# QKV stage of a fused block kernel: Y rows saved one at a time, x statistics one pass later, first z block's casts later, two tiles interleaved at the start

## The chip, the cores and the metric

One core of a Trainium2 chip runs the whole kernel. The metric is the device time of one execution in microseconds (us), lower is better. Engines are named as in the profile: PE is TensorE (matmuls and transposes), DVE is VectorE, ACT is ScalarE, POOL is GpSimd, and SP is SyncE, whose queue issues nearly all DMA transfers of this stage. Each engine works through its own instructions in program order.

## The reference, cut to what matters

```python
x = A_x                                    # 2048 tokens x 576
xn = _layernorm(x)
qkv = xn @ wqkv                            # 576 x 1728: the QKV stage
A = local_dilated_attention(qkv) @ wo      # 32 heads, window 8, dilation 2
h  = _gelu(_layernorm(xn) @ w1)            # the mixing stage's first matmul
x1 = xn + shift_mix(h) @ w2
B  = x1 + _gelu(_layernorm(x1) @ w3) @ w4  # 576 -> 4608 -> 576
return x + A + B
```

The change touches only the normalisation of x, the product with wqkv, and the preparation of z, the second normalisation of x, for the w1 product that follows.

## The kernel before, in words

Every float32 product is made from rounded parts: an operand is cast to a high part ("hi", by ACT), the rest is found by subtraction ("lo", by DVE), and hi·hi, hi·lo and lo·hi are summed in PSUM. The instruction order of each engine is the order of the Python statements; there is no scheduler. Tokens come in 16 tiles of 128. `Y[:, t, :]` holds tile t of x, and its normalised form overwrites it.

**Start.** `load_x(t)` and `load_cg(cg, ...)` put x tiles and column groups of wqkv (288 columns each) on SP's queue. For each tile `stats_x(t)` (DVE L110 to L112, then a power on POOL, L113), `norm_x(t)` (DVE L120) and `tails(t)` (POOL L292: a copy of the last columns) give the normalised tile; `turn_x(t)` and `turn_tail(t)` (PE L300, L304) transpose it, `cast_x` makes hi (ACT L311) and lo (DVE L312). The weight group is split by `hi_main` (ACT L251), `lo_main` (DVE L254) and `split_tail` (ACT L259, lo at L260). `q_head(t)` is the first 12 of a tile's 14 matmuls (PE L393), `q_tail(t)` the last two and the copy out by ACT (`q_leave`, L398). Within the 14, the first six need hi of x and of the weights and the first half of the weights' lo, numbers 6 and 7 the second half of that lo, 8 to 11 the lo of x, and the last two the tails of both.

**Units.** Then 36 units of 14 matmuls run, each a tile times a column group (`q_plain`), numbered as in `units`; the table `plan` attaches preparation work to unit numbers. Each unit's result takes one of two PSUM banks until ACT has copied it out.

**Passes.** Tiles 6 to 15 are done in five passes p = 3 to 7 of two tiles each, with a seven-product scheme: per pass three column groups of seven steps, so 21 steps, numbered 0 to 20 (the last pass has 23), each of seven matmuls (`seven`, L596). `plan[k]` holds what is issued after step k. Results leave through `leave`: ACT copies them (L605) into one of five `stg` buffers, or DVE adds them (L607) to one of five `keep` buffers (which ACT filled before, L623 and L629), and SP sends each buffer to `qkvd` (L381). While pass p computes, pass n = p + 1 is prepared: `low2` after step 3 and `up2` after step 7 transpose the two next tiles on PE (L300, L304) and form their sums, on ACT (L354) and DVE (L356, L361 to L363). The scratch space of those sums is three rows of Y, given by `raw_s`:

```python
t = {3: 13, 4: 13, 5: 0, 6: 5, 7: 5}[p]
return (Y[:, t:t + 3, :].rearrange("p a c -> p (a c)")[:, :1536]
```

So the sums of pass 5 overwrite rows 0 to 2 of Y, and those of passes 6 and 7 rows 5 to 7. These rows hold normalised x that is needed later; `away(k0, k1)` sends them to DRAM (`ysp`, L562) before, and after the pass 7 sums `back` reads them again. The same table also places `z_turn(t)` (ACT L557 scales the tile into z, DVE L129 and L130 transpose it into the one tile `ST`) and, after four of them, `put(("z", b))`: four DMAs of ST to DRAM (L137). In pass 7 `get(("z", 0))` reads the first z block (L142), `split_x` casts it (ACT L149, L150, L155) and finds its lo (DVE L151, L156), and `split_w1` splits a slice of w1 (L168, L169). The mixing stage's matmuls (L734) begin right after pass 7.

Of the kernel before, what the change touches and what calls it, by code (L numbers as in the profile page):

```python
# [8 lines left out]
F32 = mybir.dt.float32  # L9
# [48 lines left out]
def fused_block(ctx, tc, x, wqkv, wo, w1, w2, w3, w4, out):  # L58
# [188 lines left out]
    def flat(v):  # L247
        return v.rearrange("p o s c -> p o (s c)")
# [4 lines left out]
    def lo_main(raw, b, o, k):  # L253
        dve.tensor_tensor(WB[b][:, o + k, 1:3, :], raw[:, k, 1:3, :],  # L254
                          WB[b][:, o + k, 3:5, :].bitcast(F32), op=ALU.subtract)
# [46 lines left out]
    def turn_tail(t, ps):  # L302
        for k in range(2):
            pe.transpose(ps[:, k, 0:128], tl[t][:, 128 * k:128 * (k + 1)], ident)  # L304
# [23 lines left out]
    def plain_x(t):  # L328
        return x_ops(("q", t // 4)), 2 * (t % 4)
# [102 lines left out]
    for i in range(24):  # L432
# [8 lines left out]
    x0 = plain_x(0)[0]  # L441
# [63 lines left out]
    def upper(p):  # L505
# [149 lines left out]
    for p in range(3, 8):  # L655
        n = p + 1
        if n < 8:
            q4 = 4 * (p - 3)
            zs = (q4 + 1, q4 + 2, q4 + 3, q4) if p == 4 else range(q4, q4 + 4)
            plan = {k: ((z_turn, t),) for k, t in zip((9, 10, 16, 17), zs)}  # L660
            plan.update({0: ((norm_x, 2 * n),), 2: (), 3: ((low2, n),), 4: ((tails, 2 * n),),
                         7: ((up2, n),), 8: ((lambda n=n: cast_upper(n, two[n]),),),
                         14: ((cast_s, n, 0),), 15: ((cast_s, n, 1), (cast_s, n, 2))})
            plan[17] += ((put, ("z", p - 3)),)
            if n < 7:
                plan[2] = ((stats_x, 2 * n + 3),)
                plan[4] += ((stats_x, 2 * n + 2),)
                plan[17] += ((norm_x, 2 * n + 3), (tails, 2 * n + 3))
            plan[11] = {3: ((scales, 4, 6),), 4: ((away, 5, 8), (scales, 8, 10)),
                        5: ((load_w1,), (scales, 12, 14)), 6: ()}[p]  # L670
            plan[18] = {3: ((load_x, 13), (load_x, 12), (away, 0, 3)),
                        4: ((load_x, 15), (load_x, 14), (away, 3, 5))}.get(p, ())
        else:
            zx = xring
            plan = {3: ((lambda: get(("z", 0), ring_block(("z", 0))),),),
                    12: ((lambda: split_x(zx["z", 0], 2),),),
                    14: ((open_w1,), (split_w1, 0)),
                    15: ((lambda: split_x(zx["z", 0], 3),),),
                    18: ((lambda: split_x(zx["z", 0], 1),),)}
# [1061 lines left out]
```

## Time and profile before

| | |
|---|---|
| three runs | 1305.28, 1302.47, 1303.38 us; median 1303.38 us |
| profiled execution | 1301.31 us, span 1299.5 us |
| mean granted TensorE clock | 0.988 |
| PE busy | 1265.0 us, 97% of the span |
| DVE, ACT, POOL busy | 72%, 59%, 20% of the span |
| QKV stage | from the start to 214.39 us, where the mixing stage's first matmul starts |

The profile's second part cuts the span into 40 slices of about 32 us and gives each engine's busy share in tenths. PE has its only clear dips in the first slice and in the slices from 97 to 162 us, all in the QKV stage. The view of waits sums up, for each engine, what released it after idle time; the timeline gives single instructions with their start, duration and the idle time before them; the view of windows gives busy times, granted clock and DMA traffic in a stretch. In a row such as `[7.54 <-DVE Y L356]` the engine had stood idle for 7.54 us until line 356 on DVE had finished. For SP the second column is the time from the first issue to the end of the last.

### The profile page before, as it was taken

The page shows a single profiled execution, that of the slowest core. Times are in us where ns is not written, and L with a number is a line of the kernel's source. Part 1 is how long each engine was busy: PE and PEld are TensorE (multiplying, and loading weights), DVE is VectorE, ACT ScalarE, POOL GpSimd, SP SyncE. Part 2 cuts the span into 40 slices and gives each one's busy share as a digit, 9 for nine tenths or more (in the row PEclk, how much of TensorE's full clock was granted, in tenths as well). Part 3 has the DMA queues.
Part 4 walks back from the last instruction along what each step waited for, and adds up shares of the span by engine and source line. Part 5 has one row for each costly group of instructions (what it writes and reads, how often), then busy time and mean ns, then how long its engine had stood idle before and what let it go on. Part 6 is the DMA issues. An engine that isn't in the chain of part 4 may idle for free.

```text
span 1299.5 us, 21014 instructions
## 1 busy us (share of the span) xinstructions
PE 1265.0 (97%) x7819; PEld 1166.5 (90%) x7819; DVE 932.0 (72%) x1205; ACT 765.2 (59%) x1276; POOL 264.5 (20%) x408
## 2 busy tenths in 40 slices
PE   7997899999999999999999999999999999999999
PEld 7997898899889899999889999999989999999898
DVE  5875554677738798999557998998998884455341
ACT  3554455634644554554767777777757777677730
POOL 2212100011132121112113322222123223222100
PEclk9998899999999999999999999999999999999999
DMA  6736687536788879668849889878957868899982
GB/s 183 180 84 145 170 189 182 162 100 175 193 215 190 204 152 214 123 150 202 195 84 219 181 182 225 179 153 200 282 99 164 168 125 166 187 220 214 255 254 82
DMA packets 208654, 228.92 MB, mean 176 GB/s; under 512 B 80920, under 2 KB 142328, under 8 KB 208424
## 3 DMA queue, kind: packets, MB, share of 16 engines
q1 hardware_dynamic: 175800, 160.79, 43.3%
q0 software_dynamic: 32752, 66.80, 31.9%
q8 instruction: 61, 1.00, 0.3%
q14 instruction: 41, 0.34, 0.1%
HBM read 127.71 MB, written 110.23 MB: 183 GB/s over the span
## 4 chain that ended last, share of the span: by engine, by line
PE 64%; DVE 2%; ACT 2%; DMA 1%; issue 1%; SPq 0%; DVEq 0%; ACTq 0%
PE ps L1139 31%; PE cc L1401 19%; PE p L1103 9%; PE ps L183 4%; DMA td0T<-xn 1%; DVE po L1017 1%; DMA xt<-xn 1%; DVE xt L868 0%; DVE w3st L1236 0%; DVE c L1097 0%; PE p L1708 0%; ACT Y L1144 0%; ACT xt L1198 0%; DVE L L1020 0%; DVE Y L1150 0%
## 5 line engine op out<-in xcount | busy, mean ns | idle before, releaser
L1139 PEld LDWEIGHTS ps<-w,c 128*128 128x128 f32 x3456 | 478.7, 189 | 22.3 <-ACT ev L1144 2.2
L1139 PE MATMUL ps<-w,c 128*128 128x288 f32 x3456 | 489.7, 297 | 6.6 <-ACT ev L1144 2.0
L1145 POOL DMA_DIRECT2D yd<-Y x154 | 138.0, 899 | 395.6 <-ACT Y L1144 327.6
L1097 DVE TENSOR_TENSOR c<-Y,c 128x512 fp32r<-128x512 f32 x144 | 98.8, 687 | 97.2 <-ACT Y L1086 95.8
L1144 ACT COPY Y<-ps 128x576 f32<-128x576 f32 x154 | 97.8, 636 | 76.2 <-PE ps L1139 66.0
L1401 PE MATMUL cc<-xt,w3s 128*128 128x512 f32 (+1 forms) x504 | 127.7, 393 | 1.0 <-DVE Y L1411 1.0
L1401 PEld LDWEIGHTS cc<-xt,w3s 128*128 128x128 f32 (+1 forms) x504 | 92.2, 188 | 19.1 <-DVE Y L1411 1.4
L1147 ACT COPY Y<-ps 128x576 f32<-128x576 f32 x92 | 58.9, 640 | 66.3 <-PE ps L1139 64.8
L1401 PE MATMUL cc<-x1n,w3a 128*128 128x512 f32 (+1 forms) x336 | 86.7, 397 | 0.5 <-ACT cc L1604 0.5
L1017 DVE TENSOR_TENSOR po<-q,k 128x1152 f32<-128x1152 f32 (+1 forms) x48 | 84.2, 1755 | 1.0
L1020 DVE TENSOR_REDUCE L<-po 128x64 f32<-128x1152 f32 (+1 forms) x48 | 84.0, 1750 | 0.8
L1085 ACT ACTIVATE c<-p 128x512 fp32r<-128x512 f32 x48 | 28.6, 597 | 86.7 <-PE p L1103 86.6
L1411 DVE TENSOR_TENSOR Y<-cc,Y 128x512 f32<-128x512 f32 x49 | 33.7, 687 | 59.2 <-ACT Y L1407 55.1
L993 DVE TENSOR_TENSOR po<-v,L 128x1152 f32<-128x1152 f32 x56 | 75.4, 1353 | 0.9
L393 PE MATMUL p<-wb,xt 128*128 128x288 f32 (+1 forms) x504 | 72.2, 302 | 0.1
L1401 PEld LDWEIGHTS cc<-x1n,w3a 128*128 128x128 f32 (+1 forms) x336 | 61.3, 190 | 12.0 <-ACT cc L1604 0.7
L393 PEld LDWEIGHTS p<-wb,xt 128*128 128x128 f32 (+1 forms) x504 | 69.0, 192 | 1.2 <-DVE xt L449 0.3
L596 PE MATMUL ca<-wb,xt 128*128 128x288 f32 x420 | 64.4, 305 | 3.7 <-DVE keep L607 2.9
L997 DVE TENSOR_TENSOR po<-po 128x1152 f32<-128x1152 f32 x49 | 66.4, 1355 | 0.9
L596 PEld LDWEIGHTS ca<-wb,xt 128*128 128x128 f32 x420 | 60.6, 198 | 4.4 <-DVE keep L607 3.4
L1120 ACT COPY ps<-Y 128x576 f32<-128x576 f32 x92 | 59.4, 646 | 4.4 <-DVE Y L1150 2.3
L113 POOL TENSOR_TENSOR rs<-rs,mhalf 128x1 f32<-128x1 f32 x32 | 18.8, 588 | 200.5 <-DVE mv L116 109.8
(256 smaller groups left out, 2155.8 us busy)
## 6 DMA issues: line engine op xcount, KB each, us to landing
yd<-Y POOLq DMA_DIRECT2D x156, 288.0 KB, 6.1
Y<-in_B_w_dram SPq DMA_DIRECT2D x29, 576.0 KB, 6.0
w3st<-in_B_w_dram SPq DMA_DIRECT2D x56, 256.0 KB, 8.0
qkvd<-stg SPq DMA_DIRECT2D x66, 144.0 KB, 2.9
yd<-ev POOLq DMA_DIRECT2D x26, 288.0 KB, 6.5
w3st<-in_B_w_dram SPq DMA_DIRECT2D x92, 64.0 KB, 7.9
xd<-st SPq DMA_DIRECT2D x16, 320.0 KB, 4.9
xd<-big SPq DMA_DIRECT2D x16, 320.0 KB, 7.3
```

The source lines that it names most:

```text
L393: pe.matmul(ps[:, :QB], xo[:n, o + k, a, :], W[:n, w + k, v, :], start=i == 0, stop=i == len(PLAIN) - 1)
L596: pe.matmul(ps[:, :QB], xo[:n, XO[x], a, :], W[:n, OP[w], v, :], start=start and i == 0, stop=stop and i == len(HALVES) - 1, skip_group_ch ...
L993: dve.tensor_tensor(dst, vv, Lf[:, :, w:w + 1].to_broadcast([128, TPP * GH, HD]), op=ALU.mult)
L997: dve.tensor_tensor(o, o, dst, op=ALU.add)
L1017: dve.tensor_tensor(dst, qf[:, None, :].to_broadcast([128, n, TPP * GC]), win, op=ALU.mult)
L1020: dve.tensor_reduce(Lw[:, w:w + n, :], dst.rearrange("p w (x d) -> p w x d", d=HD), axis=AX.X, op=ALU.add)
L1097: dve.tensor_tensor(h[:, 1, :], g, h[:, 0, :].bitcast(F32), op=ALU.subtract)
L1103: pe.matmul(ps, W3[f][:, w, :], x1n[b][:, a, :], start=n == 0, stop=n == len(PAIRS) - 1)
L1139: pe.matmul(ps[:, k, :HF], h[:, col], w[:, p, k * HF:(k + 1) * HF], start=n == 0 and not seed, stop=n == len(seq) - 1, skip_group_check=True)
L1144: act.copy(e.rearrange("p (h c) -> p h c", h=2), ps[:, :, :HF])
L1145: pool.dma_start(yd[t], e, accum_op=ALU.add)
L1401: pe.matmul(ps, WX[w][:k, v, SLOT[w], :], area[sb][xk][:k, a, :], start=onto is None and i == 0, stop=last and i == len(HALVES) - 1, skip_ ...
```

## The change

1. *Start.* The second half of the first weight group's lo moves from DVE to POOL, `stats_x(2)` moves ahead of tile 1's lo on DVE, and the matmuls of tiles 0 and 1 are interleaved: six and six, the tail transposes, then the rest. `turn_tail(2)` moves behind the matmuls of tile 2.
2. *Units 29 to 34.* The splits of two weight groups that stood behind units 34 and 35 move to 29 and 31, and the casts of pass 3's sums one unit later.
3. *Passes 3 to 6.* Every row of Y gets its own `away`, placed after its `z_turn`, in pass 3 for rows 0 to 2 and in pass 4 for 5 to 7. The statistics of the next x tiles move from steps 2 and 4 to step 11 and to step 2 of the pass that follows, and their normalisation with them. Pass 6 sends its z block after step 14, not 17.
4. *Pass 7.* The casts of the first z block move from steps 12, 15 and 18 to 15, 17 and 20.

```diff
-    act.copy(flat(x0[:, 0:2, 3:5, :]), turns[0][:, :, 128:384])
+    cast_x(0)
     hi_main(r0, 0, 0, 1)
-    lo_main(r0, 0, 0, 1)
-    dve.tensor_tensor(flat(x0[:, 0:2, 1:3, :]), turns[0][:, :, 128:384],
-                      flat(x0[:, 0:2, 3:5, :]).bitcast(F32), op=ALU.subtract)
+    lo_main(r0, 0, 0, 1, pool)
+    stats_x(2)
     cast_x(1)
-    pq = {}
+    split_tail(r0, 0, 0, pool)
+    pq = {t: psa.tile([128, 512], F32, name="p1", tag="a") for t in range(2)}
...
-    q_head(0)
-    turn_tail(0, turns[0])
-    turn_tail(1, turns[1])
-    split_tail(r0, 0, 0, pool)
-    cast_x(0, True)
-    cast_x(1, True)
-    q_head(1)
+    for t in range(2):
+        q_part(pq[t], t, 0, 0, 6)
+    for t in range(2):
+        turn_tail(t, turns[t])
+        cast_x(t, True)
+    q_part(pq[0], 0, 0, 8, 12)
+    q_part(pq[0], 0, 0, 6, 8)
+    q_part(pq[1], 1, 0, 6, 12)
     load_cg(1, raw_rows(10))
-    stats_x(2)
     norm_x(2)
     tails(2)
+    stats_x(3)
     q_tail(0)
     turn_x(2)
-    stats_x(3)
     q_tail(1)
     cast_x(2)
-    turn_tail(2, turns[2])
     norm_x(3)
     tails(3)
     q_head(2)
+    turn_tail(2, turns[2])
...
-            28: ((stats_x, 9),), 29: ((norm_x, 9), (load_x, 10)),
-            30: ((lambda: cast_upper(3, two[3]),),), 31: ((cast_s, 3, 0),),
-            32: ((cast_s, 3, 1),), 33: ((cast_s, 3, 2), (stats_x, 8)),
-            34: ((split_t, 2, False),), 35: ((split_t, 2, True),)}
+            28: ((stats_x, 9),), 29: ((split_t, 2, False), (load_x, 10)),
+            30: ((lambda: cast_upper(3, two[3]),), (norm_x, 9)), 31: ((split_t, 2, True),),
+            32: ((cast_s, 3, 0),), 33: ((cast_s, 3, 1),), 34: ((cast_s, 3, 2), (stats_x, 8))}
...
-            plan = {k: ((z_turn, t),) for k, t in zip((9, 10, 16, 17), zs)}
-            plan.update({0: ((norm_x, 2 * n),), 2: (), 3: ((low2, n),), 4: ((tails, 2 * n),),
...
-            plan[17] += ((put, ("z", p - 3)),)
+            for k, t in zip({3: (9, 10, 14, 17), 6: (9, 10, 11, 14)}.get(p, (9, 14, 16, 17)),
+                            (q4 + 1, q4 + 2, q4 + 3, q4) if p == 4 else range(q4, q4 + 4)):
+                at(k, z_turn, t)
+            at(14 if p == 6 else 17, put, ("z", p - 3))
+            if p > 3:
+                at(0, norm_x, 2 * n + 1)
+                at(0, tails, 2 * n + 1)
+                at(2, stats_x, 2 * n)
+            at(3, low2, n)
+            at(4, norm_x, 2 * n)
+            at(4, tails, 2 * n)
...
             if n < 7:
-                plan[2] = ((stats_x, 2 * n + 3),)
-                plan[4] += ((stats_x, 2 * n + 2),)
-                plan[17] += ((norm_x, 2 * n + 3), (tails, 2 * n + 3))
-            plan[11] = {3: ((scales, 4, 6),), 4: ((away, 5, 8), (scales, 8, 10)),
-                        5: ((load_w1,), (scales, 12, 14)), 6: ()}[p]
-            plan[18] = {3: ((load_x, 13), (load_x, 12), (away, 0, 3)),
-                        4: ((load_x, 15), (load_x, 14), (away, 3, 5))}.get(p, ())
+                at(11, stats_x, 2 * n + 3)
...
+            if p == 3:
+                for t, k in enumerate((9, 10, 14)):
+                    at(k, away, t, t + 1)
+                at(11, scales, 4, 6)
+                at(18, load_x, 13)
+                at(18, load_x, 12)
+            if p == 4:
+                for t, k in ((5, 9), (6, 14), (7, 16)):
+                    at(k, away, t, t + 1)
+                at(17, away, 3, 5)
...
-                    12: ((lambda: split_x(zx["z", 0], 2),),),
-                    14: ((open_w1,), (split_w1, 0)),
-                    15: ((lambda: split_x(zx["z", 0], 3),),),
-                    18: ((lambda: split_x(zx["z", 0], 1),),)}
+            at(14, open_w1)
+            at(14, split_w1, 0)
+            at(15, lambda: split_x(xring["z", 0], 2))
+            at(17, lambda: split_x(xring["z", 0], 3))
+            at(20, lambda: split_x(xring["z", 0], 1))
```

The changed text shifts the lines of the passes: L562 becomes L560, L596 L594 and L607 L605.

SP's queue around the end of pass 3, before (`xd<-st` is the put of a z block, `Y<-in_A_x_dram` the loads of x tiles 13 and 12, `ysp0` to `ysp2` the rows 0 to 2 of Y, `stg` and `keep` results on their way to `qkvd`):

```order
L381 DMA qkvd_85<-stg_1278 128x4x72
L381 DMA qkvd_85<-keep_1199 128x4x72
L381 DMA qkvd_85<-stg_1324 128x4x72
L381 DMA qkvd_85<-keep_1258 128x4x72
L381 DMA qkvd_85<-stg_1369 128x4x72
L137 DMA xd_1389<-st_1148 32x20x128 x4
L381 DMA qkvd_85<-keep_1292 128x4x72
L210 DMA Y_71<-in_A_x_dram 128x576 x2
L562 DMA ysp0_1161<-Y_71 128x576
L562 DMA ysp1_1162<-Y_71 128x576
L562 DMA ysp2_1163<-Y_71 128x576
L381 DMA qkvd_85<-stg_1418 128x4x72
```

and now:

```order
L381 DMA qkvd_85<-stg_1268 128x4x72
L560 DMA ysp0_1161<-Y_71 128x576
L560 DMA ysp1_1162<-Y_71 128x576
L381 DMA qkvd_85<-keep_1193 128x4x72
L381 DMA qkvd_85<-stg_1321 128x4x72
L381 DMA qkvd_85<-keep_1248 128x4x72
L560 DMA ysp2_1163<-Y_71 128x576
L381 DMA qkvd_85<-stg_1371 128x4x72
L137 DMA xd_1387<-st_1148 32x20x128 x4
L381 DMA qkvd_85<-keep_1283 128x4x72
L210 DMA Y_71<-in_A_x_dram 128x576 x2
L381 DMA qkvd_85<-stg_1410 128x4x72
```

The three rows of Y now stand ahead of the four z DMAs instead of behind the x loads; the x loads keep their place.

DVE from the end of pass 3 into pass 4, before (`pp` is the PSUM tile of the next tiles' transposes; the L110 rows are the statistics of x tile 13):

```order
L607 TENSOR_TENSOR keep_1292<-cc0_1159,keep_1292 128x288
L607 TENSOR_TENSOR keep_1349<-ca1_1336,keep_1349 128x288
L120 TENSOR_SCALAR Y_71<-Y_71,mv0_77,rs0_80 128x576
L110 BN_STATS bn_83<-Y_71 128x6 x2
L111 BN_AGGR mv0_77<-bn_83 128x2
L112 TENSOR_SCALAR rs0_80<-mv0_77 128x1
L323 TENSOR_TENSOR xt_1483<-pp_1475,xt_1483 128x256
L325 TENSOR_TENSOR xt_1483<-pp_1475,xt_1483 32x128
L356 TENSOR_TENSOR Y_71<-pp_1475,Y_71 128x384
```

and now (the first L110 rows are those of tile 10, which was loaded long before):

```order
L605 TENSOR_TENSOR keep_1351<-ca1_1333,keep_1351 128x288
L120 TENSOR_SCALAR Y_71<-Y_71,mv0_77,rs0_80 128x576
L110 BN_STATS bn_83<-Y_71 128x6 x2
L111 BN_AGGR mv0_77<-bn_83 128x2
L112 TENSOR_SCALAR rs0_80<-mv0_77 128x1
L323 TENSOR_TENSOR xt_1477<-pp_1469,xt_1477 128x256
L325 TENSOR_TENSOR xt_1477<-pp_1469,xt_1477 32x128
L356 TENSOR_TENSOR Y_71<-pp_1469,Y_71 128x384
L605 TENSOR_TENSOR keep_1381<-cc1_1350,keep_1381 128x288
L120 TENSOR_SCALAR Y_71<-Y_71,mv0_77,rs0_80 128x576
```

The rows read alike, but another tile stands in them: what DVE needs ahead of L323 no longer comes from the x loads that end pass 3, and tile 13's statistics follow after step 11.

PE at the start, before (the banks `p_223` and `p_246` belong to tiles 0 and 1, `p_300` to tile 2; `ps<-ident,stg` are the tail transposes):

```order
L393 MATMUL p_223<-wb_116,xt 128x288 x12
L304 MATMUL ps<-ident,stg 128x128 x4
L393 MATMUL p_246<-wb_116,xt 128x288 x12
L393 MATMUL p_223<-wb_116,xt 128x288 x2
L300 MATMUL ps<-ident,Y 128x128 x4
L393 MATMUL p_246<-wb_116,xt 128x288 x2
L304 MATMUL ps<-ident,stg 128x128 x2
L393 MATMUL p_300<-wb_116,xt 128x288 x12
```

and now (`p_230` and `p_231` are tiles 0 and 1, `p_298` tile 2):

```order
L393 MATMUL p_230<-wb_116,xt 128x288 x6
L393 MATMUL p_231<-wb_116,xt 128x288 x6
L304 MATMUL ps<-ident,stg 128x128 x4
L393 MATMUL p_230<-wb_116,xt 128x288 x6
L393 MATMUL p_231<-wb_116,xt 128x288 x6
L393 MATMUL p_230<-wb_116,xt 128x288 x2
L300 MATMUL ps<-ident,Y 128x128 x4
L393 MATMUL p_231<-wb_116,xt 128x288 x2
L393 MATMUL p_298<-wb_116,xt 128x288 x12
L304 MATMUL ps<-ident,stg 128x128 x2
```

The count of matmuls is the same; the two tiles alternate, and tile 2's tail transposes stand behind its twelve matmuls.

More of the change, by code (lines that the diff above doesn't have):

```diff
@@ L656, in fused_block, with at @@
         n = p + 1
+        plan = {k: () for k in range(23)}
+        def at(k, f, *args):
+            plan[k] += ((f,) + args,)
         if n < 8:
             q4 = 4 * (p - 3)
-            zs = (q4 + 1, q4 + 2, q4 + 3, q4) if p == 4 else range(q4, q4 + 4)
-            plan = {k: ((z_turn, t),) for k, t in zip((9, 10, 16, 17), zs)}
-            plan.update({0: ((norm_x, 2 * n),), 2: (), 3: ((low2, n),), 4: ((tails, 2 * n),),
-                         7: ((up2, n),), 8: ((lambda n=n: cast_upper(n, two[n]),),),
-                         14: ((cast_s, n, 0),), 15: ((cast_s, n, 1), (cast_s, n, 2))})
@@ new lines, in fused_block @@
+            at(14 if p == 6 else 17, put, ("z", p - 3))
[6 more added lines that the diff above has]
+            at(4, tails, 2 * n)
+            at(7, up2, n)
+            at(8, lambda n=n: cast_upper(n, two[n]))
+            if n < 7:
+                at(11, stats_x, 2 * n + 3)
+            at(14, cast_s, n, 0)
+            at(15, cast_s, n, 1)
```

18 lines of the change are left out of this document (13 added, 5 removed).

## The prediction

> **What bounds the kernel now.** First the page's strip of slices, then PE's waits, then windows over the places that the waits name, then the timeline of each engine there. The strip shows PE full except at the start and in the fourth and fifth slices, where the granted clock dips:
>
> ```profile
> PE   7997899999999999999999999999999999999999
> PEclk9998899999999999999999999999999999999999
> ```
>
> PE's waits up to 215 us (total, times, longest):
>
> ```profile
> PE pp L300 <- DVE Y L356: 12.4, 2, 7.5
> PE ps L304 <- DVE xt L312: 3.0, 2, 1.8
> PE ca L596 <- DVE keep L607: 2.9, 2, 2.6
> PE ps L300 <- DVE Y L120: 2.1, 2, 1.7
> PE ca L596 <- ACT cb L617: 0.8, 1, 0.8
> ```
>
> All five lie in the QKV stage, and the change touches each. After it PE hardly waits, so time won here should carry to the end. Windows from `low2` to `low2` (passes 3, 4, 5; columns: length, then busy us and instructions of PE, PEld, DVE, ACT, POOL, then clock, DMA share, GB/s):
>
> ```profile
> 91.64:111.61 19.97, 19.97 (x155) 19.97 (x154) 15.10 (x36) 11.51 (x27) 5.07 (x14) 1.00 0.37 81
> 111.61:142.90 31.29, 23.75 (x161) 23.54 (x160) 15.08 (x35) 11.43 (x27) 5.07 (x14) 0.84 0.69 174
> 142.90:170.94 28.04, 23.18 (x161) 22.97 (x160) 15.00 (x35) 11.60 (x27) 5.08 (x14) 0.88 0.83 203
> ```
>
> The first is undisturbed: 155 PE instructions in 19.97 us, so 161 take 20.74 us. Pass 4 loses 31.29 - 20.74 = 10.55 us, pass 5 7.30 us, the slow clock after each wait included. Who waits, in the timelines of SP, DVE, ACT and PE:
>
> ```profile
> 107.74 4.12 SPq L137 DMA_DIRECT2D xd<-st  x4
> 113.73 2.32 SPq L210 DMA_DIRECT2D Y<-in_A_x_dram  x2
> 116.09 1.43 SPq L562 DMA_DIRECT2D ysp<-Y  x3
> 118.89 1.01 SPq L381 DMA_DIRECT2D qkvd<-keep  x1
> 118.03 0.82 DVE L110 BATCH_NORM_STATS2 bn<-Y 128x6 f32<-128x288 f32 x2 [8.64 <-DMA Y<-in_A_x_dram]
> 121.29 0.48 ACT L354 COPY Y<-pp 128x384 f32<-128x384 f32 x1 [9.09 <-DMA ysp<-Y]
> 123.70 1.09 PE L300 MATMUL pp<-ident,Y 128*128 128x128 f32 x4 [7.54 <-DVE Y L356]
> 149.56 0.82 DVE L110 BATCH_NORM_STATS2 bn<-Y 128x6 f32<-128x288 f32 x2 [8.87 <-DMA Y<-in_A_x_dram]
> ```
>
> The z block's DMAs hold SP; the x loads leave 6 us late, the rows of Y behind them 8 us late. DVE stands at the statistics until 118.03, ACT at L354 until the rows have left at 121.29; L356 needs both, and PE's next transposes need the PSUM tile that L356 reads. Pass 5 repeats it with the x load alone.
>
> **Passes 4 and 5.** Both causes go. The rows leave in steps 9 to 14 of pass 3, ahead of the z DMAs, some 10 us before L354. Tile 13's statistics stand after step 11: `low2` of pass 4 starts at 111.61, step 11 ends 8 steps of 0.93 us (pass 7, below) and two transpose groups later; the undisturbed window has 20 steps and two groups, so a group takes (19.97 - 18.66) / 2 = 0.65 us. That is 120.4, and the load had landed by 118.03. What is late next: spills. Without three rows ahead of it the `keep` of 118.89 leaves at 117.5; it lands 3.3 us later, at 120.8:
>
> ```profile
> qkvd<-keep SPq DMA_DIRECT2D x30, 144.0 KB, 3.3
> xd<-st SPq DMA_DIRECT2D x16, 320.0 KB, 4.9
> ```
>
> ACT wants that buffer again at the end of step 10, 119.4, and PE the bank that it copies from at step 13, at 121.3: with the 0.4 us copy no idle, 0.9 if the landing counts from the row's end. In pass 7 ACT waited 1.55 us for such a buffer with PE going on (row below). I take 0.7 us per pass, nearer the second reading because SP is busy with three kinds of transfer, and as bounds 0 and, for slow landings, 2. Gain: 9.85 + 6.6 = 16.45 us.
>
> **Pass 7.**
>
> ```profile
> 187.17 2.97 PE L596 MATMUL ca<-wb,xt 128*128 128x288 f32 x21
> 189.97 2.03 PE L596 MATMUL cc<-wb,xt 128*128 128x288 f32 x14
> 204.85 2.05 PE L596 MATMUL ca<-wb,xt 128*128 128x288 f32 x7 [2.62 <-DVE keep L607]
> 214.39 0.86 PE L734 MATMUL ps<-xt,W 128*128 128x512 f32 x3
> 197.75 0.40 ACT L623 COPY keep<-cc 128x288 f32<-128x288 f32 x1 [1.55 <-DMA qkvd<-keep]
> 202.97 0.61 ACT L149 CAST xt<-xt 64x512 fp32r<-64x512 f32 x1 [2.16 <-DMA xt<-xd]
> 207.23 1.05 ACT L155 CAST xt<-xt 128x1024 fp32r<-128x1024 f32 x1
> 208.31 1.23 DVE L156 TENSOR_TENSOR xt<-xt 128x1024 fp32r<-128x1024 f32 x1 [2.27 <-ACT xt L155]
> ```
>
> Three steps take 189.97 - 187.17 = 2.80 us. Pass 7 starts one step after 187.17, at 188.10; 23 steps end at 209.55, and the mixing stage starts at 214.39: 4.85 us lost, around a 2.62 us wait for the z block. The casts now stand three steps later (2.8 us), and the put ahead of the read leaves three steps earlier, so the block is there. Next in line is DVE: after step 17 come 0.45 us (ACT's copy), the 1.05 us cast, the 1.23 us subtraction and two adds of 0.45, 3.65 us, and PE wants the second add's bank after three steps, 2.8 us. That leaves 0.9 us (0 to 1.5). Gain 3.95 us. The matmul row after 2.62 us of idle took 2.05 us, not 1.1. [...]
>
> **Start.**
>
> ```profile
> 7.62 0.87 POOL L292 COPY stg<-Y 128x256 f32<-128x256 f32 x1 [0.38 <-DVE Y L120]
> 9.62 1.41 POOL L260 TENSOR_TENSOR wb<-rawa,wb 32x576 fp32r<-32x576 f32 x1 [1.14 <-ACT wb L259]
> 14.73 0.40 POOL L292 COPY stg<-Y 128x256 f32<-128x256 f32 x1 [0.68 <-DVE Y L120]
> 7.76 0.68 ACT L251 CAST wb<-rawa 128x576 fp32r<-128x576 f32 x1
> 9.75 0.68 DVE L312 TENSOR_TENSOR xt<-ps,xt 128x512 fp32r<-128x512 f32 x1
> 12.11 0.82 DVE L110 BATCH_NORM_STATS2 bn<-Y 128x6 f32<-128x288 f32 x2
> 14.72 0.66 PE L300 MATMUL ps<-ident,Y 128*128 128x128 f32 x4 [1.70 <-DVE Y L120]
> 17.75 3.01 PE L393 MATMUL p<-wb,xt 128*128 128x288 f32 x12
> 22.85 1.44 PE L393 MATMUL p<-wb,xt 128*128 128x288 f32 x9
> ```
>
> The moved weight subtraction (128x576) has no row on POOL. Near end 1.41 us, L260's time with as many elements per partition; far end four times that, 5.64, if POOL's time went with partitions. DVE takes 0.75 us for both shapes, so I take 1.41: from 8.5, after the cast and the copy, to 9.9. Statistics of tile 2 on DVE now run from about 8.9 to 10.15, the power (0.55) ends at 10.75, the weights' tail (1.41) at 12.15. Interleaving lets six matmuls of tile 1 fill PE while POOL works; both heads end near 12.2. Then the last two matmuls of tile 0; normalisation of tile 2 (after tile 1's lo and the tails) ends near 12.3, and its transposes start at 12.5, not 14.72. Copies out and the cast follow on ACT to 14.4, so tile 2's twelve start at 14.45, not 17.75. With 3.01 us as before, then transposes, cast and lo of tile 3 (0.6, 0.6, 0.7) and its tails, tile 3's matmuls start at 19.85 instead of 22.85; with a full clock at 18.9. Gain 3.3 us, bounds 4.1 and, at 5.64 us on POOL (weights' tail at 16.4), -1.4.
>
> The copy at 7.62, issued beside a DVE subtraction with both inputs in SBUF, took 0.87 us against 0.40 later. [...]
>
> **Units 29 to 35.**
>
> ```profile
> 81.26 0.41 ACT L398 COPY stg<-p 128x288 f32<-128x288 f32 x1
> 87.13 1.43 DVE L254 TENSOR_TENSOR wb<-rawb,wb 128x576 fp32r<-128x576 f32 x2
> 77.41 10.49 PE L393 MATMUL p<-wb,xt 128*128 128x288 f32 x77
> ```
>
> A split (1.43 + 0.75 us on DVE, 1.9 on ACT) now precedes pass 3's upper sums and another stands ahead of unit 32's copy; the copy of 81.26 (unit 31) becomes about 1 us later, and unit 33 needs its bank: 35 of the 77 matmuls after 77.41, at 82.1. I charge 0.8 us (0 to 1.5), and credit the 0.8 us wait for L617, which stood behind those splits, and charge 0.1 us for tile 8's later normalisation. Net -0.1.
>
> **Sum.** 16.45 + 3.95 + 3.3 - 0.1 = 23.6 us off the profiled 1301.31 gives 1277.7. That execution is 2.1 us below the median of its runs; by the median it is 1279.8. I say 1279.
>
> **Rivals.**
> (A) As summed: 1279, by itself 1275 to 1283.
> (B) DMA becomes the limit of passes 4 and 5. Packet time is 0.83 x 28.04 = 23.3 us in pass 5, to fit into 20.74: 2.6 us too much, which at pass 7's rate (4.85 lost for 2.62 waited) costs 4.8; pass 4 has 0.69 x 31.29 = 21.6 less the three rows moved out, so only the 2 us bound. Loss against A 4.1 + 1.3, so 1284. Against: pass 5's w1 load can lag without harm.
> (C) POOL's subtraction goes with partitions: start -1.4 instead of 3.3, 1284.
> (D) Slower: the z put reads the one tile ST, and `z_turn` at step 9 of the next pass must wait for it, DVE's adds behind it. The put has 13 steps and two transpose groups, 13.4 us; it takes 4.12 + 4.9 = 9 us. Idle begins when denser traffic stretches that 1.5 times; for a loss passes 4 to 6 must each lose 8 us, a put of 21 us, 2.3 times. The packet time above exceeds the pass by 1.13 at most. 1306 there.
> (E) Everything is won, no new waits: 10.55 + 7.30 + 4.85 + 4.1 + 0.8 = 27.6, 1274 to 1275.
>
> **Numbers.** A 0.65, B 0.17, C 0.08, D 0.06, E 0.04. The time is A's. The range runs from E's 1274 to B's and C's upper part, 1288. Differences under 0.2% (2.6 us) can't be told from no change. Faster: all but D and a hundredth between, 0.93; same 0.01; slower 0.06.
>
> **What would show it.** In the profile after: no wait of PE over 2 us for L356 in passes 4 and 5, `low2` to `low2` 20.7 to 22 us at a clock above 0.95; ACT waiting for `qkvd<-keep` in passes 4 and 5; the mixing stage some 23 us earlier, under 1 us of PE idle in pass 7; tile 3's matmuls near 19.5 us; the POOL subtraction near 1.4 us. I am wrong if statistics at step 11 still wait for x loads, if PE idles behind ACT's L605 or L629, or if later stages show new PE waits that eat the gain.

## The result and the profile after

The changed kernel takes 1280.95 us (median of four runs, 1279.85 to 1285.26), the kernel before in the same session 1302.93 us (1301.42 to 1305.28): a ratio of 0.984, 95% interval 0.981 to 0.986. Five more runs in a later session gave a median of 1282.25 us and a ratio of 0.985 (0.982 to 0.987). The forecast was 1279 us, with 1274 to 1288 as its range.

The strip of slices and the longest of PE's waits up to 215 us (one of 1.4 us at the very beginning, in both kernels, left out), in the profile after (span 1278.1 us; lines after the change stand two lower in this stage, so L596 is now L594, L607 is L605, L617 is L615, L623 is L621, L629 is L627, L562 is L560):

```profile
PE   8999899999999999999999999999999999999998
PEclk9999999999999999999999999999999999999999
```

```profile
PE ca L594 <- ACT keep L627: 3.5, 1, 3.5
PE p L393 <- ACT xt L311: 1.0, 1, 1.0
PE ps L304 <- POOL rs L113: 0.8, 1, 0.8
```

The waits for L356 are gone. The largest that is left is one wait of 3.5 us, behind a copy into a `keep` buffer. The windows say in which pass (from `low2` to `low2` of passes 3, 4 and 5, then pass 6 to the first matmul of pass 7, then pass 7 to the mixing stage; same columns as before):

```profile
88.11:108.63 20.52, 20.40 (x155) 19.96 (x154) 14.40 (x34) 11.47 (x27) 5.82 (x14) 1.00 0.47 122
108.63:129.88 21.25, 21.12 (x161) 20.86 (x160) 14.79 (x35) 11.56 (x27) 6.35 (x14) 1.00 0.97 209
129.88:156.47 26.59, 22.89 (x161) 22.44 (x160) 14.86 (x35) 11.36 (x27) 3.51 (x9) 0.94 0.93 217
156.47:174.02 17.55, 17.44 (x133) 17.18 (x132) 11.74 (x25) 10.49 (x24) 2.02 (x6) 1.00 0.82 169
174.02:196.42 22.40, 21.71 (x164) 21.46 (x162) 6.99 (x11) 10.16 (x22) 0.14 (x2) 1.00 0.94 200
```

Pass 4 fell from 31.29 to 21.25 us. Pass 5 hardly moved: 26.59 after 28.04. Of its 5.85 us over the undisturbed 20.74, PE stood idle for 26.59 - 22.89 = 3.70, and most of the rest is the slow clock that followed (0.50 from 143.88 to 147.29; in the repeat below the pass took 156.76 - 129.96 = 26.80 us). Place by place, against the prediction's terms (the start by tile 3's matmuls, the units by the first transposes of `low2`):

| term | forecast gain | measured |
|---|---|---|
| start | 3.3 | 22.85 - 19.54 = 3.31 |
| units 29 to 35 and pass 3 | -0.1 | 3.53 - 3.31 = 0.22 in the units, 19.97 - 20.52 = -0.55 in pass 3 |
| pass 4 | 9.85 | 31.29 - 21.25 = 10.04 |
| pass 5 | 6.6 | 28.04 - 26.59 = 1.45 |
| pass 6 | 0 | 17.16 - 17.55 = -0.39 |
| pass 7 | 3.95 | 26.29 - 22.40 = 3.89 |
| to the mixing stage's start | 23.6 | 214.39 - 196.42 = 17.97 |

The row for the start rests on tile 3's matmuls, in the changed kernel:

```profile
19.54 4.73 PE L393 MATMUL p<-wb,xt 128*128 128x288 f32 x33
```

So the forecast of the time was better than its sum, by luck: the stage gave 5.6 us less than summed. The profiled time fell by 21.5 us, of which 3.4 us came behind the start of the mixing stage (1085.1 us from there to the end, now 1081.7), where nothing was changed. Two questions were left: what holds pass 5, and whose those 3.4 us are. Here is pass 5, from the timelines of SP, ACT and PE of the changed kernel:

```profile
126.61 4.15 SPq L137 DMA_DIRECT2D xd<-st  x4
130.81 3.61 SPq L560 DMA_DIRECT2D ysp<-Y  x2
134.51 0.41 SPq L381 DMA_DIRECT2D qkvd<-keep  x1
134.97 1.34 SPq L210 DMA_DIRECT2D Y<-in_A_x_dram  x2
136.88 0.45 SPq L381 DMA_DIRECT2D qkvd<-keep  x1
137.92 0.40 ACT L621 COPY keep<-cc 128x288 f32<-128x288 f32 x1 [3.02 <-DMA qkvd<-keep]
143.19 0.40 ACT L627 COPY keep<-ca 128x288 f32<-128x288 f32 x1 [3.15 <-DMA qkvd<-keep]
143.65 3.56 PE L594 MATMUL ca<-wb,xt 128*128 128x288 f32 x14 [3.46 <-ACT keep L627]
```

The change puts the last two rows of Y, 3 and 4, directly behind the z block's four DMAs in SP's queue (step 17 of pass 4), where they had stood behind the x loads; the list of changes further up does not name this move. SP is busy with the block and these rows from 126.61 to 134.42, and the transfer of a `keep` buffer to `qkvd` (called a spill below) comes out behind them. ACT, which wants the buffers again, waits twice for 3 us: at 137.92 for the spill of 134.51, and at 143.19 for that of 136.88. Only the second wait holds PE, and its spill is slow as well as late: 6.3 us from its issue to the copy behind it, where the prediction's row had a median of 3.3 us from issue to landing.

### The profile page after: what moved, and what is told of

It reads as the page before. It is cut to its first block, busy times and chain, and to the rows that moved or that the text cites. A ratio compares the mean times of both kernels' runs of the same rounds, so it can differ in the third digit from the quotient of the medians.

```text
span 1278.1 us, 21013 instructions
## 1 busy us (share of the span) xinstructions
PE 1258.9 (99%) x7819; PEld 1159.5 (91%) x7819; DVE 930.2 (73%) x1204; ACT 766.7 (60%) x1276; POOL 268.3 (21%) x409
## 4 chain that ended last, share of the span: by engine, by line
PE 62%; DMA 3%; ACT 3%; DVE 2%; issue 1%; SPq 1%; DVEq 0%; ACTq 0%; POOLq 0%
PE ps L1165 30%; PE cc L1427 19%; PE p L1129 9%; PE ps L183 4%; DMA xt<-td1T 1%; DMA x1n<-xn 1%; DMA td0T<-xn 1%; DVE po L1043 1%; DVE xt L894 0%; DVE w3st L1262 0%; ACT Y L1170 0%; PE p L1734 0%; DVE c L1123 0%; ACT Y L1112 0%; ACT xt L1224 0%
## 5 line engine op out<-in xcount | busy, mean ns | idle before, releaser
L1170 ACT COPY Y<-ps 128x576 f32<-128x576 f32 x154 | 98.0, 637 | 75.0 <-PE ps L1165 65.4
L594 PE MATMUL ca<-wb,xt 128*128 128x288 f32 x420 | 62.9, 301 | 4.2 <-ACT keep L627 3.5
L594 PEld LDWEIGHTS ca<-wb,xt 128*128 128x128 f32 x420 | 58.9, 193 | 4.8 <-ACT keep L627 3.7
```

What stands on the lines that cost most here:

```text
L594: pe.matmul(ps[:, :QB], xo[:n, XO[x], a, :], W[:n, OP[w], v, :], start=start and i == 0, stop=stop and i == len(HALVES) - 1, skip_group_ch ...
L1170: act.copy(e.rearrange("p (h c) -> p h c", h=2), ps[:, :, :HF])
```

## The experiments

Two theories of pass 5: Q, the place of the two rows in SP's queue makes the spills late, and the five `keep` buffers turn that into idle PE; D, the prediction's rival B, the DMA engines are simply full (a share of 0.93 to 0.97 in the windows), wherever a transfer stands. All edits are against the changed kernel unless said.

**Rows 3 and 4 elsewhere.**

```diff
             if p == 4:
-                at(17, away, 3, 5)
...
             if p == 5:
-                at(11, load_w1)
+                at(9, away, 3, 4)
+                at(14, away, 4, 5)
...
             if p == 6:
+                at(9, load_w1)
```

The w1 load moves along, from pass 5 into pass 6; the next experiment leaves it in place.

> Rows 3 and 4 of Y leave in pass 5 (steps 9 and 14) instead of pass 4's step 17, and the w1 load stands in pass 6. Theory Q (the two rows behind the z block in SP's queue make pass 5's spills land late, ACT waits for a keep buffer, PE for ACT): pass 5, 26.59 us in the changed kernel, falls to 21.4 to 22.5; pass 4 stays at 21.25 within 0.3; pass 6 (17.55) stays or grows by at most 0.5; the time is 4 to 5 us under the changed kernel's 1281, so 1276 to 1277. Rival D (the core's DMA engines are simply full in passes 4 to 6, wherever a row stands): the loss moves on, pass 5 shrinks but pass 6 or 7 grows by as much, and the time stays within 1.5 us of 1281.

Its passes 4 and 5 in windows:

```profile
108.55:129.81 21.26, 21.14 (x162) 20.88 (x160) 14.78 (x35) 11.52 (x27) 6.36 (x14) 1.00 0.98 209
129.81:151.92 22.11, 21.39 (x162) 20.94 (x161) 14.85 (x35) 11.43 (x27) 3.50 (x9) 1.00 0.94 194
```

Pass 5 took 22.11 us instead of 26.59, and passes 6 and 7 together 40.18 instead of 39.95: the loss is gone, not moved on. The DMA share of pass 5 is what it was (0.94). The time was 1277.35 us (1276.19 to 1280.62; ratio to the kernel before 0.981, 0.979 to 0.984). Q's numbers, not D's.

**The same bytes in another order.**

```diff
-                at(17, away, 3, 5)
                 at(18, load_x, 15)
                 at(18, load_x, 14)
+                at(19, away, 3, 4)
+                at(20, away, 4, 5)
```

> Rows 3 and 4 leave at steps 19 and 20 of pass 4, behind the two x loads, instead of at step 17 ahead of them: the same bytes within about 3 us, another order in SP's queue. Theory Q (place in the queue): the spill of 134.5 and the x loads leave some 3 us earlier; ACT's waits shrink to under 1.5 us each and pass 5 falls from 26.59 to 22 to 24, the time by 3 to 4 us. Rival D (the bytes in these 10 us are too many for the DMA engines in whatever order): the spills land as late as now, pass 5 stays at 25.5 to 27.5 and the time within 1.5 us of 1281.

Its passes 4 and 5:

```profile
109.14:130.59 21.45, 21.33 (x162) 20.92 (x161) 14.77 (x35) 11.53 (x27) 6.27 (x14) 1.00 0.96 207
130.59:153.45 22.86, 21.39 (x162) 20.93 (x160) 14.85 (x35) 11.43 (x27) 3.50 (x9) 1.00 1.10 251
```

Pass 5 now has a higher DMA share than in the changed kernel, 1.10 against 0.93, and loses far less: 22.86 us. The spill of 134.51 leaves at 131.55 here, right behind the block; of ACT's two waits one is left, of 2.09 us, and PE waits 1.24 instead of 3.46. The second spill and the copy behind it, from the timelines of SP and ACT:

```profile
136.83 0.46 SPq L381 DMA_DIRECT2D qkvd<-keep  x1
141.69 0.40 ACT L627 COPY keep<-ca 128x288 f32<-128x288 f32 x1 [2.09 <-DMA qkvd<-keep]
```

The time was 1279.23 us (1277.67 to 1279.97). Theory D falls as it was put: with as many bytes in the pass, their order made 3.7 us, 2.2 of them in PE's wait and 1.4 in the clock behind it (the 14 matmuls took 2.12 us instead of 3.56). Of those 2.2 us the later issue is the smaller part. Counted from the pass's first transposes the second spill leaves at 7.00 us in the changed kernel and at 6.24 here, but it takes 6.3 us there and 4.9 here until the copy runs. The later landing is thus the larger part; what makes it slow is not shown.

**One more `keep` buffer.** It takes the place of one of the five `stg` buffers.

```diff
-        return qpool.tile([128, QB], F32, name="stg", bufs=5)
+        return qpool.tile([128, QB], F32, name="stg", bufs=4)
...
-            z5 = q2pool.tile([128, QB], F32, name="keep", bufs=5)
+            z5 = q2pool.tile([128, QB], F32, name="keep", bufs=6)
...
-            z = q2pool.tile([128, QB], F32, name="keep", bufs=5)
+            z = q2pool.tile([128, QB], F32, name="keep", bufs=6)
```

> One more keep buffer (6) and one less staging buffer (4), nothing else. If the count of keep buffers is what turns late spills into idle PE, ACT's two waits of 3 us shorten by about one spill interval (some 3 us): pass 5 falls from 26.59 to 22 to 23.5, the time to some 1277.5. If PE would have been held by the late spills in another way (staging buffers, the banks behind the copies), the waits show up at the staging copies and the time stays at 1281 or above.

The timeline of this kernel, one row of ACT and one of PE:

```profile
146.10 0.40 ACT L603 COPY stg<-cb 128x288 f32<-128x288 f32 x1 [3.52 <-DMA qkvd<-stg]
34.91 19.76 PE L393 MATMUL p<-wb,xt 128*128 128x288 f32 x133 [1.69 <-ACT stg L398]
```

Pass 5 fell to 22.23 us with the queue untouched, within the 22 to 23.5 expected: the count of buffers is what turns a late spill into idle PE. The spills still come late, and ACT now waits 3.52 us for a staging buffer, but PE has work until then. The time stayed at 1281.15 us all the same, since the four staging buffers cost 3.4 us earlier (the first `low2` at 91.54 instead of 88.11), in the units, where PE waits for the copy out behind the spills: 1.69 us in the row above, and most of the rest is the slow clock behind it (1.65 us more of busy PE for the same matmuls). The expectation of 1277.5 had left that out.

**The two causes of before apart.** The statistics back ahead, the rows still one by one:

```diff
-            if p > 3:
-                at(0, norm_x, 2 * n + 1)
-                at(0, tails, 2 * n + 1)
-                at(2, stats_x, 2 * n)
...
-                at(11, stats_x, 2 * n + 3)
+                at(2, stats_x, 2 * n + 3)
+                at(4, stats_x, 2 * n + 2)
+                at(17, norm_x, 2 * n + 3)
+                at(17, tails, 2 * n + 3)
```

> The changed kernel with only the statistics of x back at steps 2 and 4 of passes 3 to 6 (and the normalisations at 17), the rows of Y still leaving one by one. Theory (each of the two causes holds DVE or ACT by itself): DVE stands at the statistics until the x load has landed, 7 to 9 us after the pass's first transposes, and L356 behind it keeps PE from its next transposes: pass 4 grows from 21.25 to 26 to 30 us, pass 5 from 26.6 to 28 to 32, the time is 1288 to 1296. Rival (the rows were the real cause, the statistics only stood in the same place): passes 4 and 5 stay within 1.5 us of 21.25 and 26.59, the time within 2 us of 1281.

The rows back in groups, the statistics still late (and rows 3 and 4 behind the x loads, as before the change):

```diff
             if p == 3:
-                for t, k in enumerate((9, 10, 14)):
-                    at(k, away, t, t + 1)
+                at(18, away, 0, 3)
...
             if p == 4:
-                for t, k in ((5, 9), (6, 14), (7, 16)):
-                    at(k, away, t, t + 1)
-                at(17, away, 3, 5)
+                at(11, away, 5, 8)
+                at(18, away, 3, 5)
```

> The changed kernel with only the rows of Y back in groups (0 to 2 after the x loads of pass 3, 5 to 7 at step 11 and 3, 4 after the x loads of pass 4), statistics still late. Theory (ACT's L354 waits for rows 0 to 2, which land 9 to 11 us after pass 4's first transposes, and PE's next transposes behind it): pass 4 grows from 21.25 to 28 to 31.5 us; pass 5, whose rows 3 and 4 now stand behind the x loads, falls from 26.59 to 22 to 24; the time is 1284 to 1288. Rival (the statistics alone were the cause of pass 4's loss): pass 4 stays under 23, and the time falls to 1277 to 1279 by pass 5.

With the statistics ahead, DVE's timeline and the windows of passes 4 and 5:

```profile
117.39 0.82 DVE L110 BATCH_NORM_STATS2 bn<-Y 128x6 f32<-128x288 f32 x2 [10.26 <-DMA Y<-in_A_x_dram]
149.62 0.82 DVE L110 BATCH_NORM_STATS2 bn<-Y 128x6 f32<-128x288 f32 x2 [12.46 <-DMA Y<-in_A_x_dram]
```

```profile
109.89:139.76 29.87, 23.20 (x162) 22.75 (x160) 14.88 (x35) 11.44 (x27) 5.14 (x14) 0.89 0.63 153
139.76:172.87 33.11, 23.98 (x162) 23.53 (x161) 14.89 (x35) 11.54 (x27) 3.52 (x9) 0.85 0.73 174
```

With the rows in groups, ACT's timeline and the same windows:

```profile
117.92 0.48 ACT L354 COPY Y<-pp 128x384 f32<-128x384 f32 x1 [8.74 <-DMA ysp<-Y]
```

```profile
108.58:140.22 31.64, 23.60 (x161) 23.39 (x160) 14.85 (x35) 11.25 (x27) 5.62 (x14) 0.84 0.66 169
140.22:165.87 25.65, 22.90 (x162) 22.45 (x161) 14.95 (x35) 11.57 (x27) 3.51 (x9) 0.93 1.02 229
```

In pass 4 each cause alone brings back nearly the whole loss: 29.87 and 31.64 us, where both together cost 31.29 (and 30.46 in a second profile of the kernel before, below). The waits run side by side, DVE's for x and ACT's for the rows, so half of this part of the change would have bought next to nothing in pass 4. The times were 1295.74 us (1292.56 to 1300.45), inside what was expected, and 1291.93 us (1291.07 to 1295.25), above the 1284 to 1288 expected: pass 5 came out at 25.65, not 22 to 24. There the two rows stand behind the x loads, but in one piece ahead of the next `keep` spill, and PE waited 2.52 us for the same copy, with a clock of 0.50 behind it; in the experiment with the same bytes in another order a spill stood between them. There the second spill left 6.24 us into the pass and the copy behind it ran 4.9 us later; here it left at 6.73 and took 5.7 us. So what stands between two spills counts in both, the issue and the landing.

With the statistics ahead pass 5 is even longer than in the kernel before (33.11 against 28.04): the x loads stand behind the block and the two rows, and DVE waits 12.46 us for them, where it waited 8.87 before the change; 28 to 32 had been expected. By these rows it is the same misplacement, paid through another wait.

**Pass 7's two parts.** The casts back at their old steps, the put of the last z block still early:

```diff
-            at(15, lambda: split_x(xring["z", 0], 2))
-            at(17, lambda: split_x(xring["z", 0], 3))
-            at(20, lambda: split_x(xring["z", 0], 1))
+            at(12, lambda: split_x(xring["z", 0], 2))
+            at(15, lambda: split_x(xring["z", 0], 3))
+            at(18, lambda: split_x(xring["z", 0], 1))
```

> The changed kernel with only the first z block's casts in pass 7 back at steps 12, 15 and 18; the put of the last z block still three steps earlier in pass 6. Theory (two parts, the earlier put and the later casts, each bring about half): the read leaves SP at 7.25 us into pass 7 and lands 5.9 us on, 1 us behind the cast at the end of step 12, and the big subtraction stands in front of DVE's adds as before: pass 7's stretch to the mixing stage grows by 1.5 to 3 us against the changed kernel's 22.39. Rival (the earlier put alone brought the gain of this pass): it grows by less than 0.7 us. Rival (the casts' place alone did): it grows by 3.5 us or more, back to what the kernel before lost.

And the put back, the casts late:

```diff
-            at(14 if p == 6 else 17, put, ("z", p - 3))
+            at(17, put, ("z", p - 3))
```

> The changed kernel with only the put of the last z block (pass 6) back at step 17; pass 7's casts stay late. Theory S (each of the two parts is enough by itself: the early put lets the block land before the old casts, the late casts come after the old landing): the read leaves SP some 2 us later than now, lands near 15 us into pass 7, when the cast at the end of step 15 starts, and the stretch from pass 6's first transposes to the mixing stage, 39.95 us in the changed kernel, grows by less than 0.7 us. Theory P (the earlier put alone brought the gain, as the experiment with early casts would also allow): it grows by 2.5 us or more, towards the 43.45 of the kernel before.

From pass 6's first transposes to the mixing stage the kernel before takes 43.45 us (43.77 in its second profile) and the changed kernel 39.95. With the casts early it took 196.42 - 155.98 = 40.44, with the put late 196.98 - 156.93 = 40.05 us. My first theory, that each part brings about half, was wrong: each alone brings nearly all, 3.0 and 3.4 of 3.5 us (the repeat of the changed kernel took 39.86). In neither does ACT wait for the block, as it did before for 2.16 us. The rows of the read and of the first cast on it, from the timelines of SP and ACT, with the casts early and with the put late:

```profile
181.06 1.05 SPq L142 DMA_DIRECT2D xt<-xd  x2
186.44 0.62 ACT L149 CAST xt<-xt 64x512 fp32r<-64x512 f32 x1
```

```profile
182.56 1.04 SPq L142 DMA_DIRECT2D xt<-xd  x2
190.17 0.62 ACT L149 CAST xt<-xt 64x512 fp32r<-64x512 f32 x1
```

The times, 1283.04 us (1279.49 to 1284.79) and 1282.7 us (1282.02 to 1283.03), can't be told from the changed kernel's.

**The start alone**, put into the kernel before (its edit is the first two pieces of the diff of the change, up to tile 2):

> The kernel before with the start alone changed (interleaved first tiles, split on POOL, statistics of tile 2 a group on; nothing from unit 4 on). The prediction's term: tile 3's matmuls start near 19.5 us instead of 22.85, and the first chain of pass 3 comes 3.3 us earlier; passes 4, 5 and 7 lose what they lost before; the time is 3.3 us under the kernel before, some 1299.5. Rival: the earlier start is given back at a later wait for weights or x loads, and the time stays within 1 us of 1303.

The time was 1297.89 us (ten runs, 1294.17 to 1302.12), a ratio of 0.997 (0.995 to 0.998): 4.2 us less, 2 to 6 by the interval, as the term of 3.3 says. In the profiled run only 1.4 us had arrived at the first `low2` (90.23 against 91.64), since this run's weights came later: its ACT begins the first cast of them at 7.52 us, the kernel before at 5.71. From the timelines of ACT and PE of this kernel, the cast and the start of tile 3's matmuls:

```profile
7.52 0.67 ACT L251 CAST wb<-rawa 128x576 fp32r<-128x576 f32 x1 [5.49 <-DMA rawa<-in_A_wqkv_dram]
20.61 23.27 PE L393 MATMUL p<-wb,xt 128*128 128x288 f32 x168
```

**Both kernels once more.**

> The changed kernel once more, without an edit. What is asked: whether the 3.1 us won behind the start of the mixing stage (1081.7 us from there to the end, against 1085.1 in the kernel before) belongs to the change, and whether pass 5's slow clock after its wait is there each time. If the change brings it: 1081 to 1082.5 again. If it is scatter of the landings in the MLP stage, as the other experiments' 1081.9 to 1086.4 with the same code there suggest: any value in that span. Pass 5: 26.6 with a clock of 0.5 after the wait, or some 25.1 without; the mixing stage starts at 195 to 197; the time's median is 1280 to 1283.

> The kernel before once more, without an edit, for a second profile: whether its passes 4, 5 and 6 to 7 (31.29, 28.04 and 43.45 us) repeat. By the kernel with the start alone changed, whose passes have the same code (30.62, 27.55, 42.13), a scatter of about 1 us each is expected, and the mixing stage starting at 211.5 to 214.5.

The mixing stage starts at 196.62 us in the changed kernel and at 216.23 in the kernel before, whose passes took 30.46, 29.27 and 43.77 us; the start at 216.23 lies past the span I had given, 1.1 us of it at the first `low2` already (92.74). From there to the end the changed kernel took 1281.1 - 196.62 = 1084.5 us and the kernel before 1297.8 - 216.23 = 1081.6: the other way round than in the first pair (1081.7 and 1085.1). Over all profiles this part takes 1081.6 to 1086.4 us. A large piece of it is one PE wait in the MLP stage and the clock behind it (0.50 from 354.86 to 358.27 us in the kernel before), first of the changed kernel, then of its repeat:

```profile
333.90 1.86 PE L1165 MATMUL ps<-w,c 128*128 128x288 f32 x12 [0.76 <-ACT ev L1170]
```

```profile
336.02 3.11 PE L1165 MATMUL ps<-w,c 128*128 128x288 f32 x12 [2.00 <-ACT ev L1170]
```

ACT's copy (L1170) stands behind another instruction of ACT that waited 1.39 us for the landing of a DMA in the first and 2.62 us in the second. The kernel before waits at the same place 1.97 us in its first profile and 0.77 in its second, and in both kernels the profile with the short wait has the short rest. The 3.4 us behind the mixing stage do not belong to the change.

**A version with the findings.** Rows 3 and 4 and w1 as in the first experiment, and:

```diff
-            at(4, norm_x, 2 * n)
+            at(2 if p == 3 else 4, norm_x, 2 * n)
...
-            at(17, lambda: split_x(xring["z", 0], 3))
+            at(17, lambda: split_x(xring["z", 0], 3, None, pool))
```

The last line puts the subtraction of that part of the split on POOL.

> Rows 3 and 4 and the w1 load later as in the first experiment; tile 8's normalisation at step 2 instead of 4 of pass 3; in pass 7 one subtraction of 128x1024 of the z block's split on POOL instead of DVE. By the sum: 4.3 us as measured at the mixing stage, up to 0.5 us in pass 3 (20.5 back to 20.0), 0.7 us in pass 7 (PE's wait for DVE's add goes): the mixing stage starts near 191 instead of 196.4, the time is some 1276. Rival: POOL's subtraction, 2.5 us by the 1.42 us for 576 elements, or a conflict with DVE beside it, delays the mixing stage's first operand, and the 0.7 us turns into a loss of 0.5 or more there.

The windows of pass 3, of pass 5 and of passes 6 and 7 together, and POOL's row in pass 7:

```profile
88.03:108.15 20.12, 20.12 (x155) 20.01 (x154) 13.88 (x33) 11.44 (x27) 5.85 (x14) 1.00 0.48 125
129.42:151.25 21.83, 21.39 (x161) 20.94 (x160) 14.83 (x35) 11.42 (x27) 3.50 (x9) 1.00 0.91 196
151.25:190.32 39.07, 38.97 (x294) 38.59 (x293) 16.73 (x35) 20.07 (x46) 4.48 (x9) 1.00 1.01 229
```

```profile
187.34 2.40 POOL L156 TENSOR_TENSOR xt<-xt 128x1024 fp32r<-128x1024 f32 x1 [29.21 <-ACT xt L155]
```

Each part paid as expected: pass 3 has 20.12 us instead of 20.52, pass 5 21.83, and the last two passes 39.07 instead of 39.95, with no PE wait in pass 7. POOL's subtraction took 2.40 us and was done before the mixing stage needed it. The mixing stage starts at 190.32, and the time is 1274.72 us (1274.46 to 1279.26; ratio to the kernel before 0.980, 0.978 to 0.982): faster than both.

## Why the prediction held, point by point

- *What bounds the kernel.* Right: the waits lay in the QKV stage, and what was taken off there, 18.0 us in the first pair of profiles and 19.6 in the second, reached the end. Two sessions give 22.0 and 19.9 us on the whole (1302.93 - 1280.95 and 1302.12 - 1282.25), by which PE being full behind the stage is borne out, with the MLP stage's scatter of some 5 us between profiles on top. That 1279 came within 2 us is luck in part: of the 5.6 us that the stage fell short of its sum, 3.4 were made up by this scatter.
- *Pass 4.* Right in mechanism and size (9.85 forecast, 10.04 measured): both waits gone, 0.5 us left of the 0.7 allowed. The allowance was for late spills, though, and 0.3 of the 0.5 us come from elsewhere (pass 6, below). That the two causes overlap wholly, so that neither part pays alone, the prediction did not say.
- *Pass 5.* The step that failed: "I take 0.7 us per pass ... and as bounds 0 and 2" was worked out on the spill of 118.89 in pass 4 and carried over to pass 5. It measured 5.85, and a sign that the prediction had named for being wrong came true: PE idled 3.46 us behind ACT's L629 (now L627). The mechanism named as next, late spills and ACT waiting for `qkvd<-keep`, is the one that came, but the working never placed rows 3 and 4, which the change moves in SP's queue from behind the x loads to behind the z block. Summed from rows that stood there, the block's 4.12 us of issue, a spill at 1.0, and two rows at 1.43 / 3 each, it would at least have shown this pass to be the tight one, though not the size: the two rows took 3.61 us to issue, not 0.95, and the spill that PE waited for took 6.3 us instead of 3.3. The runs put the size on the order in the queue (3.7 us) and on the five buffers (4.4 us), either of which removes most of it; the slow clock that came with the wait, 1.4 us, is in both figures.
- *Rival B* of the prediction gave the right pass and nearly the right loss (4.1 us more than A in pass 5; 5.15 measured) for the wrong reason: the DMA engines' share was 0.97 in pass 4, which lost 0.5 us, and 1.10 in the experiment where pass 5 took 22.86 us. The share of packet time shows no limit in these runs; who stands behind whom made 3.7 us. Behind the z block and the two rows one spill took 6.3 us, where the kernel before has a median of 3.3, so some of B's thought may hold there, but what makes a landing slow is not shown.
- *Pass 7.* Size right (3.95 forecast, 3.89 measured), and so was the wait that takes its place, DVE's second add:

```profile
194.44 1.20 PE L594 MATMUL ca<-wb,xt 128*128 128x288 f32 x7 [0.69 <-DVE keep L605]
```

  0.95 us is left there, 0.9 was allowed. The two reasons given, later casts and an earlier put, are each enough by themselves.
- *Start.* Right (3.3 and 3.31), by two errors that cancel: tile 2's transposes came at 13.51, not 12.5, since the statistics of tile 2 waited 0.48 us for x and PE 0.8 us behind them; but its twelve matmuls took 1.87 us at the full clock, where 3.01 had been put in for 19.85 (in the kernel before the clock was 0.50 from 16.94 to 20.35). The profile puts PE's wait down to the power on POOL, which ended at 11.31. These tail transposes of tile 1 do not read it; DVE's lo of tile 1, which reads the PSUM tile that they write, stood behind the statistics and ended at 11.28. The agreement to 0.01 us is chance: in the second pair of profiles the start gained 23.96 - 19.68 = 4.28 us.

```profile
8.88 1.43 POOL L254 TENSOR_TENSOR wb<-rawa,wb 128x576 fp32r<-128x576 f32 x1 [0.32 <-ACT wb L251]
11.39 1.42 POOL L260 TENSOR_TENSOR wb<-rawa,wb 32x576 fp32r<-32x576 f32 x1
12.73 0.58 DVE L120 TENSOR_SCALAR Y<-Y,mv,rs 128x576 f32<-128x576 f32 x1
```

  POOL took 1.43 us for the 128 partitions and 1.42 for the 32, so rival C falls. Tile 2's normalisation on DVE, the third row, ended at 13.31, where 12.3 had been forecast.
- *Units and pass 3.* The units' charge was too high (0.22 won in place of a small loss), tile 8's later normalisation too low (0.55 us instead of 0.1; 0.40 of it came back by step 2 instead of 4).
- *Pass 6* had no term and lost 0.39 us. Most of it stands ahead of the second transposes, which come 4.66 us behind the first now (156.47 to 161.13) and came 4.39 behind them before (170.94 to 175.33):

```profile
161.13 0.63 PE L300 MATMUL pp<-ident,Y 128*128 128x128 f32 x4
```

  They read the tile that L120 on DVE normalises, at step 4 since the change, and that ended at 160.98. The same 0.3 us stand in pass 4 (4.68 us between the two) and in pass 3 (3.74 instead of 3.45), where the last version above, with the normalisation at step 2, is back at 3.45.
- *Rival D* of the prediction (the z put from the one tile ST) did not come: no wait of `z_turn` for a put stands in the profile. *Rival E* would have needed pass 5; the last version above, which won it by other means, is at 1274.72.

## What to carry to other kernels

A transfer that is moved out of a wait's way still stands somewhere in its queue: place every moved DMA against the buffers that come free behind it, pass by pass, and ask of each spill when it leaves and when it lands, since the same bytes in another order made PE wait 1.24 us or 3.46. Two waits that end at about the same time hide each other, so removing one shows little until the other goes as well (pass 4 took 31.29 us with both, 29.87 and 31.64 with one of them gone, 21.25 with neither), and two cures of one wait are not worth their sum. Where a stage behind scatters by several us, judge the change at the place where its own stage ends.

## What the runs showed of the hardware

What a wait of PE did to the clock depended on where the wait fell, not on its length alone. In four profiles with the same code in pass 5 PE stood for 3.5 to 3.7 us ahead of the same 14 matmuls, and these took 3.56, 3.37, 2.82 and 2.13 us. In the first profiles of both kernels the granted clock, 1.00 or 0.50, changes only at the lines of a grid with steps of 3.41 us: in the changed kernel it is 0.50 from 143.88 to 147.29 and again from 642.23, which is 146 steps after 143.88; in the kernel before it is 0.50 from 119.34 to 129.58, three steps, and from 150.06, six steps on, to 156.89. Here are the steps of such a grid around the wait, in windows of the changed kernel (wait of 3.46 us), its repeat (3.67) and the kernel with pass 7's casts early (3.50; its lines follow from its next slow phase, which begins at 337.54, 56 steps after 146.39):

```profile
140.47:143.88 3.41, 0.23 (x1) 0.24 (x2) 2.23 (x7) 0.69 (x2) 0.91 (x3) 1.00 0.90 178
143.88:147.29 3.41, 3.41 (x16) 3.41 (x16) 0.46 (x1) 0.02 (x1) 1.26 (x3) 0.50 0.90 218
```

```profile
141.65:145.06 3.41, 1.14 (x8) 1.14 (x9) 1.26 (x5) 0.70 (x2) 1.76 (x6) 1.00 0.83 182
145.06:148.48 3.42, 3.42 (x17) 3.42 (x16) 1.00 (x2) 1.60 (x4) 0.40 (x1) 0.50 0.96 240
```

```profile
139.56:142.98 3.42, 1.61 (x13) 1.37 (x11) 2.70 (x6) 1.60 (x4) 0.00 (x0) 1.00 1.04 220
142.98:146.39 3.41, 1.72 (x13) 1.72 (x14) 1.32 (x5) 0.70 (x2) 2.16 (x6) 1.00 0.93 191
146.39:149.81 3.42, 3.42 (x28) 3.42 (x27) 1.81 (x4) 2.92 (x7) 0.00 (x1) 1.00 0.95 305
```

In the first two kernels one step holds 3.18 and 2.27 us without PE (3.41 - 0.23 and 3.41 - 1.14), and the next step is at half the clock. In the third the wait is shared by two steps, 1.81 and 1.69 us, and the clock stays full. A step full of matmuls at 0.50 is a loss of 3.41 / 2 = 1.7 us, so the same wait cost that much besides, or nothing.

In the kernel before, six steps at the full clock, from 13.53, 115.93, 146.65, 201.26, 351.44 and 658.64 us, hold 2.49, 3.18, 2.61, 2.44, 1.87 and 2.08 us without PE, and each is followed by a step at 0.50; the step from 20.35 holds 1.22 and is followed by one at 1.00. In the changed kernel the step from 638.81 holds 1.64 us and is followed by 0.50. With the 1.81 and 1.69 us above, which were not, this puts the line near half a step, an estimate from these steps alone. The lines of the grid lie elsewhere in each of the three kernels above, and of the four waits of 3.46 to 3.67 us ahead of the 14 matmuls three were followed by a clock of 0.50 and one, of 3.50, was not.
